# Tanh for Sigmoid, softmax steps spread over two blocks, and three transposes moved from DMA to TensorE, in a fused attention and channel-mix kernel

## The chip, the cores and the metric

One Trainium2 chip, one core of it. The metric is device microseconds (us) of one execution; lower is better. Engines are named as in the profile: PE is TensorE (matmul; PEld its weight loads), DVE is VectorE, ACT is ScalarE, POOL is GpSimd, SP is SyncE, which here only issues DMAs.

## The reference

Two operations, one after the other, for 4 batches of 6208 rows with 256 channels (tau is 1).

```python
qn = q / (norm(q, axis=1) + 1e-6)            # per channel, over the rows
kn = k / (norm(k, axis=1) + 1e-6)
s = kn.transpose(0, 2, 1) @ qn / tau         # 256 x 256 for each batch
a = exp(s - s.max(-1)); a /= a.sum(-1) + 1e-9
x = v @ a
x_prev = x shifted by one row, zero in front
xk = mu_k * x + (1 - mu_k) * x_prev
xr = mu_r * x + (1 - mu_r) * x_prev
kk = maximum(xk @ w_k, 0) ** 2               # 256 -> 1024
out = 1 / (1 + exp(-(xr @ w_r))) * (kk @ w_v)
```

The softmax of a batch needs all rows of q and k of that batch; the rest goes row by row.

## The kernel before

The rows of a batch are 12 blocks of 512 and 64 rows left over. The left-over rows of all batches form a 49th block at the end. Two kinds of work run beside each other.

**Covariance.** q and k of a batch are loaded in groups of 4 units (a unit is 128 rows); the 64 left-over rows are a group of one unit, group 0. `unit_matmul` adds a unit to the 256 x 256 sum `s_ps` with two matmuls (L133). `group_norms` adds the squares of a group (`qk2`) to the channel sums `ssq_ps`, with four matmuls of 32 columns side by side (L145). Batch 0 is loaded as f32 on SP's queue (L102), cast by VectorE (L113) and squared by ScalarE (L115). Later batches are cast to bf16 by the DMA, issued from GpSimd's queue (L107), and squared by ScalarE (L120). In the trace, `qk_392` and the like on ScalarE are such squares.

**Softmax chain** (`softmax_pieces`), once per batch: `copies` (ssq out of PSUM, L161), `gather` (four matmuls into `bank`, L168, then ScalarE's Sqrt into `rn`, L170), `evac` (s_ps out of PSUM, L185), `invert` (reciprocal of rn and a diagonal `rq_d`, L173 to L176), `spread` (matmul of rq_d with ones, L182), `scale` (L188), `exp` (ScalarE, L197), `weigh` (row sums inverted, `a_sb` written, L202 and L204).

**Channel mix**, block by block. A block's v is loaded as bf16 from GpSimd's queue (`v_load`, L223) and transposed by a DMA from SP's queue (`v_transpose`, L230) into `vT`. `x_half` makes half of the transposed x (L247), which ScalarE copies out (L249). VectorE makes the difference to the row before (`delta`, L279) and the two mixtures `xk` and `xr` (L289). `up` is the projection to 1024 in eight steps (L304) with a Relu on ScalarE (L307), `square` squares it on VectorE (L313), `down` makes gate and projection for 128 rows (L328, L332) in two halves, `finish` applies Sigmoid on ScalarE (L340) and multiplies on VectorE (L341).

The order on every engine is that of the code; nothing is reordered. Ahead of the loop stand all units of batch 0, its chain, the loads of the weights and the first units of batch 1. The loop runs over i from -2 and over eight steps j: in block i stand `down` of block i, `up` of block i + 1, and `x_half` and the mixtures of block i + 2, with v transposed for block i + 4 and loaded for i + 5. Units of the next batch stand at certain steps, and a chain is taken up piece by piece, one piece a step, as soon as its batch is complete:

```python
if chain:
    chain.pop(0)()
...
if j in ((5, 7) if i == -2 else (1, 3, 4, 5, 7)) and ...:
    unit(0 if i < -1 else 2)
```

Every wait of an instruction holds all that stand behind it on the same engine or queue. PSUM tiles are shared by tag: `kT_ps` has three buffers, `vr_ps` two, `xT_ps` one; `v_bf` has five buffers, `vT` four.

Of the kernel before, what the change touches and what calls it, by code (L numbers as in the profile page):

```python
# [18 lines left out]
def kernel(  # L19
# [13 lines left out]
    nc = tc.nc  # L33
# [32 lines left out]

    mu_k_t = const.tile([P, 2], F32, name="mu_k_t")
# [13 lines left out]
    def sizes(b):  # L81
        return [1] + [S] * (NB - 1) + ([S // 2] * 2 if b == 0 else [S])

# [38 lines left out]
    def unit_matmul(b, g, s, late=False):  # L122
        rows, n = rows_of(b, g)
        t0 = g == 0
        te = g == len(sizes(b)) - 1 and s == n - 1
        if t0:

            cov[b] = (ps.tile([P, 2, C], F32, name="s_ps", tag="s_ps" if b else "vr_ps", bufs=1 if b else 2),
                      ps.tile([P, 2 * C], F32, name="ssq_ps", tag="ssq_ps" if b else "vr_ps", bufs=1 if b else 2))
        s_ps = cov[b][0]  # L130
        qk = groups[b, g][0]
        for ih in range(2):
            nc.tensor.matmul(s_ps[:, ih, :], qk[:rows, s, 1, ih * P:(ih + 1) * P],  # L133
                             qk[:rows, s, 0, :], start=t0 and ih == 0, stop=te,
                             skip_group_check=True)
        if s == n - 1 and not late:
            group_norms(b, g)

    def group_norms(b, g):
# [4 lines left out]
        for u in range(n):  # L144
            nc.tensor.matmul(ssq_ps[32 * u:32 * (u + 1)], ones[:rows, :32],  # L145
                             qk2[:rows, u].rearrange("p i c -> p (i c)"),
                             start=g == (1 if u else 0), stop=g == len(sizes(b)) - 1, tile_position=(0, 32 * u),
                             skip_group_check=True)

    def softmax_pieces(b):  # L150
# [12 lines left out]
        def gather():  # L163
# [6 lines left out]
            nc.scalar.activation(rn, bank[:, C:C + 4], AF.Sqrt)  # L170

        def invert():
            nc.vector.tensor_scalar_add(rn, rn, 1e-6)  # L173
            nc.vector.reciprocal(rn, rn)
            for h in range(2):
                nc.vector.tensor_scalar_mul(rq_d[:, h * P:(h + 1) * P], ident_f, rn[:, h:h + 1])  # L176
            if inv_tau != 1.0:
                nc.vector.tensor_scalar_mul(rk, rk, inv_tau)
# [26 lines left out]


        return [copies, gather, evac, invert, spread, scale] + ([] if bounded else [top]) + [exp, weigh]


# [16 lines left out]
    def v_transpose(i):  # L226
# [4 lines left out]
        st[i, "vT"] = vT  # L231

# [102 lines left out]
    def finish(i, s):  # L335
# [4 lines left out]
        nc.scalar.activation(res[:, s], vr_ps[:, D:], AF.Sigmoid)  # L340
        nc.vector.tensor_tensor(res[:, s], res[:, s], vr_ps[:, :D], op=OP.mult)  # L341
# [11 lines left out]
    for g in range(len(sizes(0))):  # L353
# [4 lines left out]
        if g == NB - 5:  # L358
            nc.sync.dma_start(mu_k_t, moe_mu_k.rearrange("(h p) -> p h", p=P))
            nc.sync.dma_start(mu_r_t, moe_mu_r.rearrange("(h p) -> p h", p=P))  # L360
# [43 lines left out]

    next_load()
    next_load()
    nc.gpsimd.dma_start(w_k_sb, moe_w_k.rearrange("(ko ki) f -> ki ko f", ki=P))
# [3 lines left out]
    nc.gpsimd.dma_start(w_v_sb, moe_w_v.rearrange("(fo fi) d -> fi fo d", fi=P))  # L411
    next_load()
    v_load(2)
    v_transpose(0)
    v_transpose(1)
# [15 lines left out]
    for u in early:  # L431
        unit_square(*u)
    group_norms(*early[0][:2])
    pos["sq"] += S
    pos["mm"] += S

# [3 lines left out]
    for i in range(-2, NBLK):  # L440
        for j in range(8):
# [7 lines left out]
            if chain:  # L449
                chain.pop(0)()  # L450
# [24 lines left out]
            if j == 5 and 2 <= i + 4 < NBLK - 1:  # L475
                v_transpose(i + 4)
            b = (i + 2) // NB
            if j in ((5, 7) if i == -2 else (1, 3, 4, 5, 7)) and pos["mm"] < len(units) and units[pos["mm"]][0] <= b + 1:
                unit(0 if i < -1 else 2)
# [41 lines left out]
```

## Time and profile before

| | |
|---|---|
| median of 3 runs | 558.94 us (558.53 to 561.2) |
| profiled execution | 563.61 us, its span 561.8 us |
| TensorE busy | 511.9 us (91%), mean granted clock 0.965 |
| ScalarE busy | 451.1 us (80%) |
| VectorE busy | 408.4 us (73%) |
| GpSimd busy | 98.2 us (17%) |
| DMA | 84.55 MB, mean 150 GB/s |

The span goes from the first to the last instruction; about 1.8 us of the profiled execution lie outside. A row of the timeline has the start, the length, the engine, the line, the operation with what it writes and reads, how many of them were merged, and in brackets the idle time ahead of it and what ended it. In a row of groups stand, behind the bar, the busy time in all and the mean in ns of one instruction. A row of a DMA issue ends with the time from issue to landing.

### The profile page before, as it was taken

The numbers are of one execution on the slowest core, as the hardware profiler recorded it, in microseconds if no ns is written. First come the engines' busy times: TensorE is split into PE (matmuls) and PEld (weight loads), VectorE is DVE, ScalarE is ACT, GpSimd is POOL, SyncE is SP. The second block draws the span as 40 slices with busy tenths as digits, with TensorE's granted clock in tenths as the row PEclk, the third lists the DMA queues.
The fourth block names the chain that finished last, engine by engine and source line by source line (L and its number), as shares of the span: only waits on it lengthen the run. The fifth ranks groups of instructions, "written<-read, shape, count | busy, mean of one in ns | idle before, by whom it ended". The sixth has DMA issues, their size and how long they took to land. (4 is left out here: it accounts for less than half of the span.)

```text
span 561.8 us, 9979 instructions
## 1 busy us (share of the span) xinstructions
PE 511.9 (91%) x3502; PEld 333.8 (59%) x3560; DVE 408.4 (73%) x953; ACT 451.1 (80%) x897; POOL 98.2 (17%) x140
## 2 busy tenths in 40 slices
PE   4765679999988999999988999999989999999996
PEld 1331346666655666666655666666655666666665
DVE  3552637787758777777778777777778898888984
ACT  6773768888868898888888898889879777878774
POOL 0045413124210213222310213221001010000000
PEclk9785979999989999999999999999999999999999
DMA  8989999979992699899992699899643768534122
GB/s 289 402 253 180 191 176 169 198 126 141 185 164 56 124 179 167 132 199 141 183 182 57 98 206 163 132 194 155 123 85 76 144 104 133 108 84 114 37 76 95
DMA packets 147426, 84.55 MB, mean 150 GB/s; under 512 B 55408, under 2 KB 143792, under 8 KB 147376
## 3 DMA queue, kind: packets, MB, share of 16 engines
q0 software_dynamic: 65808, 33.01, 48.7%
q1 hardware_dynamic: 81568, 50.90, 38.1%
q8 instruction: 28, 0.46, 0.4%
q14 instruction: 22, 0.18, 0.1%
HBM read 78.71 MB, written 25.43 MB: 185 GB/s over the span
## 5 line engine op out<-in xcount | busy, mean ns | idle before, releaser
L307 ACT ACTIVATE kr<-kT_ps 128x512 bf16<-128x512 f32 (+1 forms) x392 | 232.7, 596 | 46.4 <-PE kT_ps L304 31.9
L332 PE MATMUL vr_ps<-w_v_sb,kk 128*128 128x256 bf16 x1552 | 234.7, 274 | 4.2 <-DVE kk L313 2.1
L304 PE MATMUL kT_ps<-xk,w_k_sb 128*128 128x512 bf16 (+1 forms) x726 | 221.4, 380 | 2.3 <-ACT kr L307 1.6
L332 PEld LDWEIGHTS <-kk 128*128 128x128 bf16 x1552 | 152.4, 98 | 62.4 <-DVE kk L313 3.8
L313 DVE TENSOR_TENSOR kk<-kr 128x512 bf16<-128x512 bf16 (+1 forms) x392 | 155.4, 415 | 5.9 <-ACT kr L307 5.3
L341 DVE TENSOR_TENSOR res<-res,vr_ps 128x256 f32<-128x256 f32 x194 | 81.2, 419 | 90.6 <-ACT res L340 88.9
L304 PEld LDWEIGHTS <-w_k_sb 128*128 128x128 bf16 x784 | 73.9, 99 | 40.4 <-issue 12.4
L249 ACT CAST xT<-xT_ps 128x512 bf16<-128x512 f32 x95 | 55.9, 589 | 42.8 <-PE xT_ps L247 42.8
L133 PE MATMUL s_ps<-qk 128*128 128x256 bf16 (+1 forms) x392 | 75.6, 297 | 15.9 <-DVE qk L113 14.6
L328 PE MATMUL vr_ps<-w_r_sb,xr 128*128 128x256 bf16 x388 | 74.5, 274 | 4.0 <-DVE res L341 3.3
L340 ACT ACTIVATE res<-vr_ps 128x256 f32<-128x256 f32 x194 | 74.1, 382 | 3.1 <-PE vr_ps L332 2.3
L289 DVE SCALAR_TENSOR_TENSOR xr<-delta,mu_r_t,xT 128x512 bf16<-128x512 bf16 x96 | 71.4, 744 | 0.0
L289 DVE SCALAR_TENSOR_TENSOR xk<-delta,mu_k_t,xT 128x512 bf16<-128x512 bf16 x96 | 71.4, 744 | 0.0
L247 PE MATMUL xT_ps<-vT,a_sb 128*128 128x512 bf16 x192 | 58.4, 388 | 11.4 <-DMA vT<-v_bf 11.4
L328 PEld LDWEIGHTS <-xr 128*128 128x128 bf16 x388 | 38.2, 98 | 49.7 <-issue 6.5
L107 POOL DMA_DIRECT2D qk<-in_q_dram x39 | 28.9, 741 | 221.9 <-ACT qk_3346 L120 31.3
L133 PEld LDWEIGHTS <-qk 128*128 128x128 bf16 (+1 forms) x392 | 39.4, 105 | 30.9 <-DVE qk L113 19.7
L223 POOL DMA_DIRECT2D v_bf<-in_v_dram x48 | 36.4, 761 | 118.5 <-DMA vT<-v_bf 99.5
L279 DVE TENSOR_TENSOR delta<-xT 128x1024 bf16<-128x1024 bf16 x48 | 33.3, 693 | 17.0 <-ACT xT L249 16.9
L107 POOL DMA_DIRECT2D qk<-in_k_dram x39 | 28.9, 742 | 4.9 <-DMA w_v_sb<-in_moe_w_v_dram 2.9
L247 PEld LDWEIGHTS <-a_sb 128*128 128x128 bf16 x192 | 19.0, 100 | 15.8 <-issue 13.4
L145 PEld LDWEIGHTS <-ones 128*32 128x32 bf16 (+1 forms) x196 | 5.7, 94 | 14.7 <-issue 14.7
(193 smaller groups left out, 236.4 us busy)
## 6 DMA issues: line engine op xcount, KB each, us to landing
out_dram<-res SPq DMA_DIRECT2D x48, 512.0 KB, 3.9
v_bf<-in_v_dram POOLq DMA_DIRECT2D x48, 256.0 KB, 7.9
qk<-in_q_dram POOLq DMA_DIRECT2D x36, 256.0 KB, 5.6
qk<-in_k_dram POOLq DMA_DIRECT2D x36, 256.0 KB, 6.9
vT<-v_bf SPq DMA_TRANSPOSE x48, 5.6
f_110<-in_q_dram SPq DMA_DIRECT2D x1, 512.0 KB, 4.0
f_112<-in_k_dram SPq DMA_DIRECT2D x1, 512.0 KB, 5.1
f_132<-in_q_dram SPq DMA_DIRECT2D x1, 512.0 KB, 5.8
```

What stands on the lines that cost most here:

```text
L107: nc.gpsimd.dma_start(qk[:rows, :n, i, :], qk_src(t, b, g))
L133: nc.tensor.matmul(s_ps[:, ih, :], qk[:rows, s, 1, ih * P:(ih + 1) * P], qk[:rows, s, 0, :], start=t0 and ih == 0, stop=te, skip_group_che ...
L247: nc.tensor.matmul(xT_ps, a_sb[:, b, ih, dh * P:(dh + 1) * P], vT[:, :, ih, :], start=ih == 0, stop=ih == 1)
L249: (nc.vector.tensor_copy if first else nc.scalar.copy)(xT[:, dh, 1:], xT_ps)
L289: nc.vector.scalar_tensor_tensor(o[:, dh], st[i, "d"][:, dh], mu[:, dh:dh + 1], st[i, "x"][:, dh, :M], op0=OP.mult, op1=OP.add)
L304: nc.tensor.matmul(kT_ps[:, :m], w_k_sb[:, dh, fh * P:(fh + 1) * P], xk[:, dh, :m], start=dh == 0, stop=dh == 1)
L307: nc.scalar.activation(kr[:, :m], kT_ps[:, :m], AF.Relu)
L313: nc.vector.tensor_tensor(st[i, "kk"][:, fh, :m], kr[:, :m], kr[:, :m], op=OP.mult)
L328: nc.tensor.matmul(vr_ps[:, D:], xr[:, dh, s * P:(s + 1) * P], w_r_sb[:, dh, :], start=dh == 0, stop=dh == 1)
L332: nc.tensor.matmul(vr_ps[:, :D], kk[:, fh, s * P:(s + 1) * P], w_v_sb[:, fh, :], start=fh == 0, stop=fh == 7)
L340: nc.scalar.activation(res[:, s], vr_ps[:, D:], AF.Sigmoid)
L341: nc.vector.tensor_tensor(res[:, s], res[:, s], vr_ps[:, :D], op=OP.mult)
```

## The change

- The gate is made with Tanh: sigmoid(z) = (1 + tanh(z/2)) / 2. `finish` has Tanh on ScalarE and (res + 1) * vr in one scalar_tensor_tensor on VectorE; the factor 1/2 goes into w_v_sb, halved once by VectorE in block -1 of the loop.
- For batches 1 to 3 the root leaves ScalarE: VectorE copies the four columns of `bank` to `rn`, GpSimd raises them to 0.5. The chain of these batches has 16 steps instead of 8, seven or eight of them empty.
- v of blocks 0, 1 and 2 is transposed by eight TensorE transposes each, into a PSUM tile of the tag `kT_ps`, and copied out by VectorE, ScalarE and VectorE.
- Batch 0 loads its groups in the order 1, 2, 0, 3, ...; the two small mu loads go out first, from ScalarE's queue. On GpSimd's queue w_k goes ahead of the first group of batch 1, and one group fewer is loaded there ahead of the loop; v of block 2 stands ahead of the third.
- Ahead of the steady loop stand 7 units of batch 1 instead of 12; blocks 0 to 7 have six units instead of five.

```diff
+    half = const.tile([P, 4], F32, name="half")
+    nc.vector.memset(half, 0.5)
...
-            nc.scalar.activation(rn, bank[:, C:C + 4], AF.Sqrt)
+            if b == 0:
+                nc.scalar.activation(rn, bank[:, C:C + 4], AF.Sqrt)
+
+        def roots():
+            nc.vector.tensor_copy(rn, cov[b][:, C:C + 4])
+
+        def roots2():
+            nc.gpsimd.tensor_tensor(rn, rn, half, op=OP.pow)
...
+        return [copies, None, gather, roots, roots2, evac, None, invert, None, spread, None, scale,
+                None if bounded else top, exp, None, weigh]
...
+    def v_transpose_pe(i, evac):
+        v_bf = st.pop((i, "v"))
+        vT_ps = ps.tile([P, S, 2, P], BF16, name="vT_ps", tag="kT_ps", bufs=3)
+        for s in range(S):
+            for h in range(2):
+                nc.tensor.transpose(vT_ps[:, s, h], v_bf[:, s, h * P:(h + 1) * P], ident)
+        def go():
+            vT = p2.tile([P, S, 2, P], BF16, name="vT", tag="vT", bufs=4)
+            evac(vT, vT_ps)
+            st[i, "vT"] = vT
+        return go
...
-        nc.scalar.activation(res[:, s], vr_ps[:, D:], AF.Sigmoid)
-        nc.vector.tensor_tensor(res[:, s], res[:, s], vr_ps[:, :D], op=OP.mult)
+        nc.scalar.activation(res[:, s], vr_ps[:, D:], AF.Tanh, scale=0.5)
+        nc.vector.scalar_tensor_tensor(res[:, s], res[:, s], 1.0, vr_ps[:, :D], op0=OP.add, op1=OP.mult)
...
-    for g in range(len(sizes(0))):
+    nc.scalar.dma_start(mu_k_t, moe_mu_k.rearrange("(h p) -> p h", p=P))
+    nc.scalar.dma_start(mu_r_t, moe_mu_r.rearrange("(h p) -> p h", p=P))
+    for g in order(0):
...
-    v_transpose(0)
-    v_transpose(1)
...
     evac()
+    go = v_transpose_pe(0, nc.vector.tensor_copy)
     invert()
     spread()
+    go()
     unit(0)
-    early = units[pos["mm"]:pos["mm"] + S]
-    for u in early:
-        unit_matmul(*u, late=True)
     for f in rest:
         f()
     for h in range(2):
         x_half(0, h)
-    for u in early:
-        unit_square(*u)
-    group_norms(*early[0][:2])
...
+    v_transpose_pe(1, nc.scalar.copy)()
+    for _ in range(S):
+        unit(0)
...
+            if i == -1 and j == 6:
+                v_transpose_pe(2, nc.vector.tensor_copy)()
+                nc.vector.tensor_scalar_mul(w_v_sb, w_v_sb, 0.5)
...
+            if i < -1:
+                slots = ()
+            elif i == -1:
+                slots = (5, 7)
+            elif i < 8:
+                slots = (1, 2, 3, 4, 5, 7)
+            else:
+                slots = (1, 3, 4, 5, 7)
```

What this makes of the order on the engines is shown at three places. First ScalarE from the dummy Exp of batch 0's chain (`gate`) into block -1, before:

```order
L419 ACTIVATE gate<-ones 128x1
L120 ACTIVATE qk_388<-qk 64x512
L197 ACTIVATE s_sb,sm<-s_sb,rn 128x256 x2
L249 CAST xT<-xT_ps 128x512
L120 ACTIVATE qk_392<-qk 128x512 x4
L120 ACTIVATE qk_399<-qk 128x512 x2
L307 ACTIVATE kr<-kT_ps 128x512
L249 CAST xT<-xT_ps 128x512
```

and in the changed kernel:

```order
L448 ACTIVATE gate<-ones 128x1
L127 ACTIVATE qk_391<-qk 64x512
L211 ACTIVATE s_sb,sm<-s_sb,rn 128x256 x2
L281 CAST xT<-xT_ps 128x512
L261 COPY vT<-vT_ps 128x1024
L127 ACTIVATE qk_397<-qk 128x512 x4
L339 ACTIVATE kr<-kT_ps 128x512
L281 CAST xT<-xT_ps 128x512
```

The copy of block 1's vT now stands ahead of the first relu (`kr`), and two of the six squares ahead of it have moved behind.

Second, VectorE in block -1, around the last squares of block 0 (`kk`); before:

```order
L289 SCALAR_TENSOR_TENSOR xk<-delta,mu_k_t,xT 128x512
L313 TENSOR_TENSOR kk<-kr 128x512 x2
L289 SCALAR_TENSOR_TENSOR xr<-delta,mu_r_t,xT 128x512
L313 TENSOR_TENSOR kk<-kr 128x512
L241 COPY xT<-xT 128x2
```

and in the changed kernel:

```order
L345 TENSOR_TENSOR kk<-kr 128x512
L261 COPY vT<-vT_ps 128x1024
L504 TENSOR_SCALAR w_v_sb<-w_v_sb 128x2048
L345 TENSOR_TENSOR kk<-kr 128x512
L321 SCALAR_TENSOR_TENSOR xr<-delta,mu_r_t,xT 128x512
L345 TENSOR_TENSOR kk<-kr 128x512
L273 COPY xT<-xT 128x2
```

The copy of block 2's vT and the halving of w_v stand ahead of the last two squares of block 0.

Third, VectorE in the chain of batch 1, from the first to the middle step; before, all in one piece of the loop:

```order
L161 COPY ssq<-ssq_ps 128x512
L313 TENSOR_TENSOR kk<-kr 128x512
L289 SCALAR_TENSOR_TENSOR xk<-delta,mu_k_t,xT 128x512
L313 TENSOR_TENSOR kk<-kr 128x512
L289 SCALAR_TENSOR_TENSOR xk<-delta,mu_k_t,xT 128x512
L341 TENSOR_TENSOR res<-res,vr_ps 128x256
L185 COPY s_sb<-s_ps 128x512
L313 TENSOR_TENSOR kk<-kr 128x512
L173 TENSOR_SCALAR rn<-rn 128x4
L174 RECIPROCAL rn<-rn 128x4
L176 TENSOR_SCALAR rq_d<-ident_f,rn 128x128 x2
```

and in the changed kernel, from the copy of the four columns on:

```order
L181 COPY rn<-bank 128x4
L345 TENSOR_TENSOR kk<-kr 128x512
L311 TENSOR_TENSOR delta<-xT 128x1024
L374 SCALAR_TENSOR_TENSOR res<-res,vr_ps 128x256
L345 TENSOR_TENSOR kk<-kr 128x512
L321 SCALAR_TENSOR_TENSOR xk<-delta,mu_k_t,xT 128x512
L199 COPY s_sb<-s_ps 128x512
L345 TENSOR_TENSOR kk<-kr 128x512
L321 SCALAR_TENSOR_TENSOR xk<-delta,mu_k_t,xT 128x512
L374 SCALAR_TENSOR_TENSOR res<-res,vr_ps 128x256
L345 TENSOR_TENSOR kk<-kr 128x512
L187 TENSOR_SCALAR rn<-rn 128x4
```

Between the copy of `rn` (L181) and its next use (L187) now stand ten other instructions of VectorE, and GpSimd's root. Before, `rn` came from ScalarE, behind a table load. On GpSimd's queue the root stands between the v loads of blocks 12 and 13:

```order
L114 DMA qk<-in_k_dram 128x4x256
L241 DMA v_bf<-in_v_dram 128x4x256
L184 TENSOR_TENSOR rn<-rn,half 128x4
L241 DMA v_bf<-in_v_dram 128x4x256 x3
L114 DMA qk<-in_q_dram 128x4x256
```

ScalarE's row has 16 table loads before and three in the changed kernel, the last of them for the dummy Exp of batch 0's chain.

More of the change, by code (lines that the diff above doesn't have):

```diff
@@ L82, in sizes, with order @@
         return [1] + [S] * (NB - 1) + ([S // 2] * 2 if b == 0 else [S])
+    def order(b):
+        g = list(range(len(sizes(b))))
+        return [1, 2, 0] + g[3:] if b == 0 else g
     def rows_of(b, g):
@@ L123, in unit_matmul @@
         rows, n = rows_of(b, g)
-        t0 = g == 0
+        t0 = g == order(b)[0] and s == 0
         te = g == len(sizes(b)) - 1 and s == n - 1
@@ L403, in next_load @@
         pos["ld"] += 1
+    nc.gpsimd.dma_start(w_k_sb, moe_w_k.rearrange("(ko ki) f -> ki ko f", ki=P))
     next_load()
-    next_load()
-    nc.gpsimd.dma_start(w_k_sb, moe_w_k.rearrange("(ko ki) f -> ki ko f", ki=P))
     v_load(1)
@@ L449 @@
             if chain:
-                chain.pop(0)()
+                piece = chain.pop(0)
+                if piece is not None:
+                    piece()
             if 0 <= i + 1 < NBLK:
```

22 lines of the change are left out of this document (9 added, 13 removed).

## Prediction

> **What bounds the kernel now.** I read the busy totals, then the table of busy time by stretch, then TensorE's timeline at the places where that table shows gaps.
>
> ```profile
> span 561.8 us, 9979 instructions
> PE 511.9 (91%) x3502; PEld 333.8 (59%) x3560; DVE 408.4 (73%) x953; ACT 451.1 (80%) x897; POOL 98.2 (17%) x140
> ```
>
> TensorE is idle for 49.9 of 561.8 us. Each row of the next table gives a stretch, its length, the busy time of PE, PEld, DVE, ACT and POOL, the granted clock, the DMA share and GB/s.
>
> ```profile
> 10.00:20.00 10.00, 7.53 (x54) 3.68 (x52) 5.55 (x8) 8.20 (x9) 0.00 (x0) 1.00 1.02 417
> ...
> 500.00:540.00 40.00, 39.79 (x278) 27.04 (x280) 34.97 (x83) 31.71 (x65) 0.00 (x0) 1.00 0.28 78
> ```
>
> Between 10 and 20 us the DMA engines are full (1.02, 417 GB/s): loading the first q and k sets the pace. Late in the program TensorE is busy 39.79 of 40 us at full clock: there it is the bound, and nothing done for another engine can help. What can be gained is idle or slow TensorE time, and it lies in the start-up and in the softmax chains.
>
> ```profile
> 46.50:52.20 5.70, 1.08 (x6) 0.47 (x4) 0.00 (x0) 0.00 (x0) 1.65 (x3) 0.50 1.33 181
> ...
> 66.60:73.10 6.50, 1.14 (x7) 0.68 (x7) 3.10 (x8) 2.47 (x5) 1.51 (x3) 0.91 1.45 160
> 73.10:78.80 5.70, 5.46 (x22) 2.57 (x23) 0.90 (x3) 3.97 (x6) 1.48 (x2) 0.51 1.39 188
> ```
>
> Two stretches with TensorE almost idle, and after the second one 5.46 us of work at a granted clock of 0.51. TensorE's timeline (start, length, then in brackets the idle time before and its releaser) names what it waited for:
>
> ```profile
> 45.69 1.89 PE L133 MATMUL s_ps<-qk 128*128 128x256 bf16 x8 [0.99 <-DMA qk<-in_k_dram]
> 52.21 1.86 PE L247 MATMUL xT_ps<-vT,a_sb 128*128 128x512 bf16 x4 [4.64 <-DMA vT<-v_bf]
> 54.43 2.14 PE L145 MATMUL ssq_ps<-qk_392,ones 128*32 128x512 bf16 x4 [0.35 <-ACT qk_392 L120]
> ...
> 57.32 1.06 PE L304 MATMUL kT_ps<-xk,w_k_sb 128*128 128x512 bf16 x2
> 59.83 0.59 PE L247 MATMUL xT_ps<-vT,a_sb 128*128 128x512 bf16 x2 [1.45 <-DMA vT<-v_bf]
> ...
> 66.62 0.59 PE L304 MATMUL kT_ps<-xk,w_k_sb 128*128 128x512 bf16 x2 [0.20 <-ACT kr L307]
> ...
> 73.12 1.01 PE L247 MATMUL xT_ps<-vT,a_sb 128*128 128x512 bf16 x2 [5.36 <-DMA vT<-v_bf]
> ```
>
> All three waits of the first blocks are for a DMA transpose. v itself is there long before:
>
> ```profile
> 36.44 0.87 POOL L223 DMA_DIRECT2D v_bf<-in_v_dram  x1
> ...
> 40.60 0.83 POOL L223 DMA_DIRECT2D v_bf<-in_v_dram  x1
> ```
> ```profile
> v_bf<-in_v_dram POOLq DMA_DIRECT2D x1, 256.0 KB, 4.1
> ```
> ```profile
> v_bf<-in_v_dram POOLq DMA_DIRECT2D x1, 256.0 KB, 10.1
> ```
> ```profile
> vT<-v_bf SPq DMA_TRANSPOSE x1, 11.6
> ```
>
> Issue to landing: v of block 0 lands at 36.4 + 4.1 = 40.5, its transpose needs 11.6 us more because the queues are full; v of block 1 lands at 50.7.
>
> The three later chains, one stretch each:
>
> ```profile
> 153.00:177.00 24.00, 19.60 (x117) 12.19 (x118) 16.59 (x42) 18.08 (x36) 3.17 (x5) 0.93 0.65 102
> ...
> 283.00:306.00 23.00, 19.47 (x129) 12.26 (x129) 17.70 (x44) 19.69 (x38) 2.22 (x3) 1.00 0.70 117
> ...
> 408.00:432.00 24.00, 20.48 (x136) 13.01 (x138) 18.16 (x46) 19.74 (x39) 1.48 (x2) 1.00 0.43 84
> ```
> ```profile
> 160.68 1.19 PE L182 MATMUL bank<-rq_d,ones_f 128*128 128x256 f32 x2 [2.22 <-DVE rq_d L176]
> ```
>
> TensorE loses 4.4, 3.5 and 3.5 us there, and the first one also 0.07 x 24 = 1.7 us of clock: 13.1 us in all. In the order of before, ScalarE's table loads stand inside these chains:
>
> ```profile
> L340 ACT ACT_TABLE_LOAD x7 | 9.0, 1283 | 0.1
> L170 ACT ACT_TABLE_LOAD x4 | 5.1, 1283 | 0.1
> L197 ACT ACT_TABLE_LOAD x3 | 3.8, 1283 | 0.1
> ```
>
> **The change part by part.** All in us of the profiled execution, 563.61 (span 561.8, 1.8 around it); the median of the runs, 558.94, is 4.7 lower, and the gains are taken from that.
>
> (1) Loads of the first phase, +1.5.
>
> ```profile
> 0.74 0.59 SPq L102 DMA_DIRECT2D f_95<-in_q_dram  x1
> ...
> 2.00 0.59 SPq L102 DMA_DIRECT2D f_110<-in_q_dram  x1
> ...
> 14.14 0.39 SPq L359 DMA_DIRECT2D mu_k_t<-in_moe_mu_k_dram  x1
> ```
>
> The first 512 KB load now goes out at 0.74 instead of 2.00: 1.26 us of a full pipe. The two 1 KB mu loads leave SP's queue, where each took one of the turns of a phase that the DMA bounds; they go out from ScalarE's queue before it has work. Nothing gained if the pipe fills no sooner, 3 if both come in full; I take 1.5, nearest to the head of the queue.
>
> (2) First up projection earlier, +2.9. The vT copy of block 0 (128x1024 from PSUM) stands on VectorE ahead of `scale`, and eight transposes on TensorE ahead of `spread`. A 128x128 transpose isn't in the trace. Below it costs a weight load; above, a 128x256 matmul at half clock, so eight at most the 1.89 us of the row at 45.69. I take 1.9, as this stretch has half clock. A bound for the copy comes from two rows (1024 elements from SBUF; 512 from PSUM, doubled):
>
> ```profile
> L113 DVE CAST qk<-f_110 128x1024 bf16<-128x1024 f32 x1 | 0.7, 694 | 2.1 <-DMA f_110<-in_q_dram 2.1
> ```
> ```profile
> L161 DVE COPY ssq<-ssq_ps 128x512 f32<-128x512 f32 x4 | 2.7, 685 | 1.0 <-PE ssq_ps L145 1.0
> ```
>
> 0.7 to 1.4; I take 1.2. Together they delay the chain by some 0.5:
>
> ```profile
> 45.72 0.62 DVE L204 TENSOR_SCALAR a_sb<-s_sb,sm 128x256 bf16<-128x256 f32 x2
> ```
> ```profile
> 53.74 2.19 ACT L120 ACTIVATE qk_392<-qk 128x512 bf16<-128x512 bf16 x4
> ...
> 66.93 1.13 ACT L307 ACTIVATE kr<-kT_ps 128x512 bf16<-128x512 f32 x2
> ```
>
> So a_sb is ready at 46.3 + 0.5 = 46.8, four xT matmuls (1.86) end at 48.7, eight transposes of block 1 at 50.6 (its v lands no later than 50.7, and now has one group less ahead of it). ScalarE copies that vT (1024 elements, as two relus: 1.1) to 51.7, then squares four units (2.19) to 53.9; the norms follow, and the first up projection starts at 54.4 instead of 57.32. The new wait: TensorE is in order, so these norms hold it where the transposes did.
>
> (3) Block -1 of the loop, +1.5. Before, 57.32 to 66.62, 9.3 us. Now ScalarE has 8 relus, 2 xT copies and 4 squares: 14 x 0.55 = 7.7. I take 7.8.
>
> (4) The wait for block 2's transpose, +5.4 (row at 73.12), and the slow clock after it, +2.0: 5.46 us at 0.51 are 2.7 too many, but the new start has a cold stretch of its own, so between 0 and 2.7.
>
> (5) VectorE in block -1, -1.5. The vT copy (1.2) and the halving of w_v_sb (2048 bf16 elements: between 0.35, the a_sb row of 256 elements below, and 2.8, eight times it; I take 1.4, twice the cast above) stand ahead of the last two squares of block 0. Behind them wait `kk`, then the second half of block 0's first down projection. Full cost 2.6, nothing if VectorE has run ahead.
>
> (6) Units deferred, -1.8. Twelve units were done before the steady loop, now seven; five move to blocks where TensorE is the bound. Two matmuls of a unit cost 1.89/4/2 = 0.24 at full clock, plus a quarter of four concurrent norms (at most 2.14/4 at half clock): 0.24 to 0.5, I take 0.35.
>
> (7) Block 3 is the first with a DMA transpose, -0.7. Its v goes out after w_v, v2 and two to three groups, lands near 61, and its transpose takes 9 to 12 us as above: 70 to 73, needed at about 71. Between 0 and 3.
>
> (8) The later chains, +9.5. The loads of tables go (three remain, all in the first chain), Sqrt leaves ScalarE, and each step now has one or two empty steps behind it, so a result is asked for 1 to 2 us later than before. VectorE's work stays:
>
> ```profile
> L341 DVE TENSOR_TENSOR res<-res,vr_ps 128x256 f32<-128x256 f32 x194 | 81.2, 419 | 90.6 <-ACT res L340 88.9
> ...
> L204 DVE TENSOR_SCALAR a_sb<-s_sb,sm 128x256 bf16<-128x256 f32 x8 | 2.5, 350 | 0.1
> L176 DVE TENSOR_SCALAR rq_d<-ident_f,rn 128x128 f32<-128x128 f32 x8 | 2.1, 334 | 0.1
> ...
> L294 DVE SCALAR_TENSOR_TENSOR xk<-delta,mu_k_t,xl 128x256 bf16<-128x256 bf16 x2 | 1.0, 476 | 0.0
> ```
>
> Per chain three 128x512 operations (0.685), two of 0.334, two of 0.350: 3.4, and 0.5 for eight gates. A block has 18 VectorE instructions, so the 83 between 500 and 540 are 4.6 blocks of 8.7 us with 12.6% spare: 2.2 in two blocks. It is 1.7 short; I leave 1.2 of loss per chain, as some of it fits into buffers. 13.1 - 3.6 = 9.5; at worst 6, at best 13.
>
> (9) The gate as scalar_tensor_tensor, -0.3. By 476 against 419 it costs 57 ns more, 194 times: 11 us of VectorE, beside TensorE's work. The other end is 2, if the last blocks (VectorE at 34.97 of 40) feel it. Tanh itself is one activation of the same shape. The root on GpSimd:
>
> ```profile
> masks.py:199 POOL TENSOR_SCALAR_AFFINE_SELECT ident<-ident 128x128 bf16<-128x128 bf16 x1 | 0.3, 288 | 0.1
> ```
>
> No pow stands in the trace; this row, with 32 times the elements, says 0.3, above I allow 4 and take 1. VectorE has about 4 us of other rows between writing `rn` and reading it back. The v loads behind it on GpSimd's queue lose their lead over the program, but are five blocks early.
>
> Sum: 1.5 + 2.9 + 1.5 + 5.4 + 2.0 - 1.5 - 1.8 - 0.7 + 9.5 - 0.3 = 18.5. The profiled execution would be 545.1, the median 540.4.
>
> The Trainium skill ("TensorE: Matmul & The Clock Gate", section "Part 4: PE-mode transpose") gives about 275 ns for such a transpose in one kernel and says that it does not bring up the full clock. By 275 ns the sixteen of blocks 0 and 1 would be an estimated 4.4 us instead of 3.8, the sum 0.6 less.
>
> **The rivals.**
> - Clock. The stretch at 0.51 shows TensorE slow for over 5 us of dense work after a pause. If the transposes don't count as work for the clock, block -1 runs at half speed: the 2.0 of step 4 and the 1.5 of step 3 go, 544. For it: 46.5 to 52.2 stood at 0.50. Against: that was an idle stretch, and ScalarE bounds block -1. The Trainium skill (same page and section as above) states this rule.
> - Transfers. Blocks now ask for data 12 us earlier, while the DMA share is 1.4 to 1.45. If vT of block 3 or 4 and the groups (six units a block instead of five) come as late as before, the 5.4 of step 4 is paid again: 546. Against: three transposes left the queues.
> - VectorE bounds the chains. If spreading saves only the table loads and each still costs 2.8, the gain is 4.7 instead of 9.5: 545.
> - Slower: pow. If it takes longer than the 4 us of cover, VectorE stops in order, `kk` comes late and TensorE with it, three times. To eat 18.5 it must take 4 + 6.2 = 10 us; at 12 us the result is 565. Against: all GpSimd rows that compute take 0.1 to 0.3 us.
> - That tables are loaded all the same is excluded by the order of the changed program, which holds three loads.
>
> **How the numbers follow.** My forecast 58%, clock 13%, transfers 12%, VectorE 13%, pow 4%. Less than 0.5% (2.8 us) cannot be told from no change. All but the last are faster, and I keep 2% for no change and 3% for slower: 0.95, 0.02, 0.03. Range: the best ends of steps 1, 4, 5 and 8 together reach 533; two of the milder rivals together give 549 to 550. 534 to 549.
>
> **What would show it.** Right: no wait for vT in the first three blocks, first up projection near 53, second block's near 60; no table load after the first chain; TensorE idle under 2 us in each chain. Wrong: a wait of several us at the fourth block's xT; a clock near 0.5 past 60 us; VectorE waiting for GpSimd before `rn`; idle TensorE in steady blocks, where 57 ns more per gate would be felt.

## The result, and the profile after

The changed kernel takes 539.25 us (median of 4 runs, 538.85 to 539.62), the kernel before beside it 558.74 us (4 runs, 558.46 to 561.2): a ratio of 0.9642, interval 0.9613 to 0.967. Forecast were 540.4 us and 534 to 549. The profiled execution of after took 539.62 us, 0.4 above the median of its runs; that of before lay 4.7 above (563.61 against 558.94).

The page of after begins:

```profile
span 537.8 us, 10013 instructions
PE 505.4 (94%) x3525; PEld 333.8 (62%) x3584; DVE 410.0 (76%) x960; ACT 434.9 (81%) x882; POOL 101.4 (19%) x143
```

TensorE is idle for 32.4 us of the span; before it was 49.9. ScalarE is 16.2 us less busy; thirteen table loads of 1.28 us that are gone (16 before, three now) would be 16.7, and a copy of vT is new.

**Start-up.** TensorE's timeline of after, at the rows that answer to those of before:

```profile
43.35 1.05 PE L175 MATMUL bank<-thirty_83,ssq 128*128 128x1 f32 x8 [0.79 <-DVE ssq L168]
44.26 0.61 PE L257 MATMUL vT_ps<-ident,v_bf 128*128 128x128 bf16 x8
...
51.42 1.06 PE L257 MATMUL vT_ps<-ident,v_bf 128*128 128x128 bf16 x8
...
55.98 0.60 PE L336 MATMUL kT_ps<-xk,w_k_sb 128*128 128x512 bf16 x2
...
60.20 0.61 PE L257 MATMUL vT_ps<-ident,v_bf 128*128 128x128 bf16 x8
...
62.72 0.59 PE L336 MATMUL kT_ps<-xk,w_k_sb 128*128 128x512 bf16 x2 [1.21 <-ACT kr L339]
63.80 0.59 PE L279 MATMUL xT_ps<-vT,a_sb 128*128 128x512 bf16 x2
64.23 0.59 PE L336 MATMUL kT_ps<-xk,w_k_sb 128*128 128x512 bf16 x2
...
74.66 0.59 PE L279 MATMUL xT_ps<-vT,a_sb 128*128 128x512 bf16 x2
```

No `xT` matmul waits for a transpose, not that of block 2 (63.80) nor that of block 3 (74.66), whose transpose is still a DMA. The gather of the norms (43.35), though, comes later than before, where it stood at 39.92. Of before, that row and the first one behind the wait for block 2's transpose:

```profile
39.92 1.05 PE L168 MATMUL bank<-thirty_83,ssq 128*128 128x1 f32 x8 [0.79 <-DVE ssq L161]
...
73.93 1.06 PE L304 MATMUL kT_ps<-xk,w_k_sb 128*128 128x512 bf16 x2
```

The table by stretch has the same columns as in the prediction:

```profile
46.50:52.20 5.70, 3.98 (x16) 1.66 (x16) 2.02 (x6) 2.20 (x6) 3.99 (x6) 0.50 1.42 191
52.20:57.30 5.10, 3.97 (x21) 1.85 (x21) 3.06 (x7) 3.78 (x7) 2.70 (x4) 0.96 1.46 197
57.30:60.00 2.70, 2.70 (x15) 1.31 (x14) 2.60 (x6) 2.70 (x7) 1.48 (x2) 1.00 1.46 195
138.60:150.10 11.50, 11.41 (x80) 7.72 (x78) 10.07 (x26) 7.87 (x17) 7.01 (x9) 1.00 0.89 145
150.10:158.80 8.70, 8.55 (x59) 5.58 (x58) 8.66 (x23) 7.47 (x18) 0.00 (x0) 1.00 1.33 199
270.20:280.70 10.50, 10.32 (x70) 6.85 (x69) 9.30 (x25) 7.47 (x15) 6.26 (x8) 1.00 1.11 175
280.70:290.80 10.10, 9.56 (x64) 6.25 (x64) 8.82 (x24) 7.96 (x19) 0.00 (x0) 1.00 1.03 157
```

The last four rows are the first two later chains: TensorE is idle for 0.24 and 0.72 us in them, at full clock, though VectorE is busy 8.66 of 8.70 us. The clock is full from the middle of the 50s on.

**Where the time went.** A good ruler is the moment at which SP issues the store of a block's output. Three of these rows of before and then of after (blocks 0, 18 and 22; the second chain lies between the last two):

```profile
86.34 0.41 SPq L345 DMA_DIRECT2D out_dram<-res  x1
...
276.97 0.37 SPq L345 DMA_DIRECT2D out_dram<-res  x1
...
321.06 0.37 SPq L345 DMA_DIRECT2D out_dram<-res  x1
```
```profile
74.61 0.42 SPq L378 DMA_DIRECT2D out_dram<-res  x1
...
259.91 0.37 SPq L378 DMA_DIRECT2D out_dram<-res  x1
...
300.57 0.37 SPq L378 DMA_DIRECT2D out_dram<-res  x1
```

Differences of such rows, in us:

| from store to store | before | after | gain |
|---|---|---|---|
| start to block 0 | 86.34 | 74.61 | 11.73 |
| 0 to 6 (deferred units) | 62.26 | 64.00 | -1.74 |
| 6 to 9 (chain 1) | 35.18 | 28.11 | 7.07 |
| 18 to 22 (chain 2) | 44.09 | 40.66 | 3.43 |
| 30 to 34 (chain 3) | 42.20 | 38.52 | 3.68 |
| all others, to the last store | 286.80 | 286.80 | 0.00 |

The sum is 24.2, as the spans have it (24.0). It is 4.7 more than the 19.5 between the medians. A slow start of the profiled execution of before is 3.2 of that, as the first experiment shows; the rest is not traced to a place.

### The profile page after: what moved, and what is told of

Same layout as the page of the kernel before. It is cut to its first block, busy times and chain, and to the rows that moved or that the text cites. A ratio compares the mean times of both kernels' runs of the same rounds, so it can differ in the third digit from the quotient of the medians.

```text
span 537.8 us, 10013 instructions
## 1 busy us (share of the span) xinstructions
PE 505.4 (94%) x3525; PEld 333.8 (62%) x3584; DVE 410.0 (76%) x960; ACT 434.9 (81%) x882; POOL 101.4 (19%) x143
## 4 chain that ended last, share of the span: by engine, by line
PE 84%; DMA 8%; DVE 3%; ACT 2%; issue 1%; POOL 0%; SPq 0%; ACTq 0%
PE vr_ps L364 31%; PE kT_ps L336 28%; PE vr_ps L360 8%; PE xT_ps L279 8%; PE s_ps L140 6%; PE ssq_ps L152 2%; DMA f_336<-in_k_dram 2%; DMA f_248<-in_k_dram 2%; DMA f_160<-in_k_dram 1%; DMA qk<-in_k_dram 1%; DMA mu_k_t<-in_moe_mu_k_dram 1%; DVE xk L321 1%; ACT kr L339 1%; DVE kk L345 1%; DVE res L374 1%
## 5 line engine op out<-in xcount | busy, mean ns | idle before, releaser
L336 PE MATMUL kT_ps<-xk,w_k_sb 128*128 128x512 bf16 (+1 forms) x725 | 218.9, 377 | 2.9 <-ACT kr L339 1.2
L374 DVE SCALAR_TENSOR_TENSOR res<-res,vr_ps 128x256 f32<-128x256 f32 x194 | 81.5, 420 | 74.8 <-ACT res L373 72.5
L336 PEld LDWEIGHTS <-w_k_sb 128*128 128x128 bf16 x784 | 73.3, 98 | 37.7 <-issue 10.5
L140 PE MATMUL s_ps<-qk 128*128 128x256 bf16 (+1 forms) x392 | 75.1, 295 | 17.9 <-DVE qk L120 17.2
```

What stands on the lines that cost most here:

```text
L336: nc.tensor.matmul(kT_ps[:, :m], w_k_sb[:, dh, fh * P:(fh + 1) * P], xk[:, dh, :m], start=dh == 0, stop=dh == 1)
L374: nc.vector.scalar_tensor_tensor(res[:, s], res[:, s], 1.0, vr_ps[:, :D], op0=OP.add, op1=OP.mult)
```

## The experiments

**The kernel before, once more.** No edit.

> The kernel before, unchanged, for a second profile of it: the first profiled execution took 563.6 us where the median was 558.7, and the start times of its output stores show 7.1 us gained at the first of the later chains, but 3.4 and 3.7 at the other two. Theory: about 3 of the 4.9 us too many lie in the first of the later chains (a clock drop and a longer wait there), and a second profile shows that chain losing 3 to 4 us like the others, total near 558.7. Rival: the 4.9 us lie in the start-up, where the clock changes, and that chain loses 6 us again.

560.35 us, span 558.6. Its stores of blocks 0, 18 and 22:

```profile
83.14 0.40 SPq L345 DMA_DIRECT2D out_dram<-res  x1
...
273.72 0.37 SPq L345 DMA_DIRECT2D out_dram<-res  x1
...
317.80 0.37 SPq L345 DMA_DIRECT2D out_dram<-res  x1
```

Block 0 comes 3.20 us earlier than in the first profile; from 18 to 22 it is 44.08 against 44.09, and no stretch of the table behind block 0 differs by more than 0.1. The two executions differ in the start-up alone; the chains cost the same in both. The seven kernels of this document that have the chains of after (after itself, the five with other first loads, the one with DMA transposes) agree as well: 28.09 to 28.11, 40.66 to 40.67 and 38.51 to 38.73 us for the three chains. So a chain is read from one profile to about 0.2 us, while an edit to the start-up needs medians.

**DMA transposes for blocks 0 to 2 again.**

```diff
+    v_transpose(0)
+    v_transpose(1)
...
-    go = v_transpose_pe(0, nc.vector.tensor_copy)
...
-    v_transpose_pe(1, nc.scalar.copy)()
...
-                v_transpose_pe(2, nc.vector.tensor_copy)()
...
-            if j == 5 and 3 <= i + 4 < NBLK - 1:
+            if j == 5 and 2 <= i + 4 < NBLK - 1:
                 v_transpose(i + 4)
```

> The changed kernel with v of blocks 0, 1 and 2 transposed by DMA again, all else as changed. By steps 2 to 5 of the prediction the transposes are worth 2.9 + 1.5 + 5.4 + 2.0 - 1.5 = 10.3 us: 547 to 551, with waits of several us for vT ahead of the xT matmuls. Rival (transfers reordered in the queue do most of it, since v of block 2 now goes out ahead of the third group): 541 to 544.

543.1 us (541.94 to 544.03, 4 runs), 3.9 over after; ratio to before 0.9681 (0.9635 to 0.9727). TensorE's timeline has the waits back; its gather and its first row behind the wait for block 2 stand around them:

```profile
41.73 1.05 PE L175 MATMUL bank<-thirty,ssq 128*128 128x1 f32 x8 [0.79 <-DVE ssq L168]
...
51.21 1.87 PE L279 MATMUL xT_ps<-vT,a_sb 128*128 128x512 bf16 x4 [4.50 <-DMA vT<-v_bf]
...
66.74 0.78 PE L279 MATMUL xT_ps<-vT,a_sb 128*128 128x512 bf16 x2 [2.97 <-DMA vT<-v_bf]
67.32 1.06 PE L336 MATMUL kT_ps<-xk,w_k_sb 128*128 128x512 bf16 x2
```

With a third wait of 0.20 they sum to 7.7 us (11.4 in before), and the store of block 0 comes 4.6 later than in after: a wait taken away here is worth little more than half of its length. That other work then waits in its place is the likely reason, not one that a run shows.

The time lies where the rival put it, and the rival's mechanism shows in part: v of block 2 goes out at 45.14 us here and at 48.98 in before, and the wait for its transpose is 2.97 instead of 5.36 us. From the gather to the row behind that wait it is 34.01 us in before, 25.59 here and 20.88 in after. So of the 13.1 us gained in this piece, 8.4 came without the transposes, with the other edits ahead of the loop: the order on GpSimd's queue, one group and five units fewer. No run moves these one by one. Without the transposes the whole change still gains 17.9 us (561.03 for before beside it).

**Where the two small mu loads go.** Five kernels. First, mu back in the middle of SP's queue, the new group order kept:

```diff
-    nc.scalar.dma_start(mu_k_t, ...)
-    nc.scalar.dma_start(mu_r_t, ...)
...
+        if g == NB - 5:
+            nc.sync.dma_start(mu_k_t, ...)
+            nc.sync.dma_start(mu_r_t, ...)
```

> The changed kernel with the two mu loads back in the middle of SP's queue. Theory (slots): in the changed kernel SP's seventh and ninth load wait until the two slow mu loads have landed (5.1 and 6.5 us), because all hardware queues share a ring of completion slots; without them ahead of it SP goes on after six loads as fast as the loads land: last cast of batch 0 1.5 to 2.5 us earlier than 39.0, result 536.5 to 538. Rival (group order): the loss comes from the large group first; nothing gained, 539 to 539.5.

Then mu at the start as in after, but from GpSimd's queue (`nc.gpsimd.dma_start`):

> The changed kernel with the two mu loads at the very start, but issued from GpSimd's queue. Slots theory: SP's queue no longer waits for them, last cast 1.5 to 2.5 us earlier, 536 to 538. Rival (packets): the 4-byte packets themselves hold the DMA engines at the start whoever issues them, and the time stays at 538.5 to 539.5.

The old group order, mu at the start on ScalarE's queue (`order(b)` returns `g`, and the flag that starts the sum of the norms follows):

> The changed kernel with batch 0's groups in their old order 0, 1, 2, ..., the mu loads still first on ScalarE's queue. Slots theory: SP still waits for the mu loads, nothing gained or up to 0.8 lost, 539 to 540. Rival (group order): the old order alone gives back the 1.4 us that the loads are late, 537 to 538.

Mu on SP's queue behind the last load of batch 0:

> The changed kernel with the two mu loads behind the last load of batch 0 on SP's queue; they are wanted only by the mixtures of block 0, near 52 us. Packets theory (the 544 small packets hold the DMA engines for 1 to 2 us of a phase that the DMA bounds, wherever in it they stand): out of that phase they cost nothing, last cast of batch 0 ends 0.5 to 1 us before the 37.6 of the kernel with them in the middle, result 535.5 to 537, no worse than 536.8. Rival (place in the phase doesn't matter, only the wait at its head): as with them in the middle, 536.8.

Old order and mu in the middle of SP's queue, both edits undone:

> The changed kernel with both of its edits to the first loads undone: groups of batch 0 in the old order, the two mu loads in the middle of SP's queue. Each undone alone gave 537.7 (order) and 536.8 (mu). If both act on the same thing (the small packets of mu standing ahead of or beside the first large loads), this gives 536.5 to 537.5, no better than the mu edit alone. If they add, 535 to 536. If the new order is worth the 1.26 us that the earlier first full load suggests, once mu is out of the way, it gives 538, about 1.2 over the mu edit alone.

| group order | mu loads | median us (runs) | ratio to before |
|---|---|---|---|
| new (after) | first, ScalarE's queue | 539.25 (538.85 to 539.62, 4) | 0.9613 to 0.967 |
| new | first, GpSimd's queue | 539.37 (538.27 to 539.98, 4) | 0.9569 to 0.9637 |
| old | first, ScalarE's queue | 537.74 (537.5 to 538.47, 4) | 0.9546 to 0.9611 |
| old | middle, SP's queue | 537.62 (536.45 to 538.09, 6) | 0.9558 to 0.9619 |
| new | end, SP's queue | 537.1 (536.51 to 537.39, 6) | 0.9549 to 0.9611 |
| new | middle, SP's queue | 536.84 (535.98 to 538.6, 5) | 0.9535 to 0.9603 |

The median of before lay between 558.74 and 561.44 in the sets of runs behind this table, so the cleanest pair is mu from GpSimd's queue against mu in the middle, both with the new order and side by side on one chip: 2.5 us. The stretch from 4 to 8 us, of after, of mu from GpSimd's queue and of mu in the middle:

```profile
4.00:8.00 4.00, 0.00 (x0) 0.00 (x0) 1.39 (x2) 1.79 (x2) 0.00 (x0) 1.00 0.74 257
```
```profile
4.00:8.00 4.00, 1.01 (x5) 0.73 (x6) 1.39 (x2) 2.11 (x2) 0.00 (x0) 1.00 0.95 274
```
```profile
4.00:8.00 4.00, 0.82 (x4) 0.57 (x5) 1.65 (x3) 2.37 (x3) 0.00 (x0) 1.00 1.01 360
```

257 or 274 GB/s against 360: with mu at the start, whichever queue issues it, four microseconds carry some 0.3 to 0.4 MB less, about 1 us of a full pipe. The two loads are 1 KB each, but the page lists them as 544 packets, and in after they need 5.1 and 6.5 us to land.

SP also waits 1.2 + 0.9 us for their completions before it issues two later group loads; that a shared ring is the reason, as the first expectation says, no run shows. This wait does not explain the loss: from GpSimd's queue SP never waits for mu, and the time is the same. With the new order, mu at the start costs 2.4 us (539.25 against 536.84); with the old order, where a small group goes first, nothing that can be told (537.74 against 537.62). Between the orders with mu in the middle lie 0.8 us (537.62 and 536.84), with ranges that overlap. That small packets hold the DMA engines is a reading that fits, not one that a run isolates, and two results limit it. With mu at the end, behind the whole phase, nothing more is gained than in its middle (537.1 and 536.84), so inside the phase the same packets cost nothing that can be told. And with the old order the stretch from 4 to 8 us carries 314 GB/s with mu at the start and 357 without, yet no time is lost. The kernel with the new order and mu in the middle, 536.84, is faster than before and after: its highest run, 538.6, lies below the lowest of after, 538.85, though the two were not run side by side.

**Chain packed again:** its ten pieces in ten steps running, root still on GpSimd, Tanh kept.

```diff
-        return [copies, None, gather, roots, roots2, evac, None, invert, None, spread, None, scale,
-                None if bounded else top, exp, None, weigh]
+        return [copies, gather, roots, roots2, evac, invert, spread, scale] + ([] if bounded else [top]) + [exp, weigh]
```

> The changed kernel with the later chains in ten consecutive steps, without the empty ones; Tanh and the root on GpSimd stay. Theory (the distance between steps matters): VectorE comes to the scaled diagonal 1 to 2 us after the copy, ahead of GpSimd's 1.03 us, and TensorE waits at the first and the second small matmul, 1.5 to 3 us a chain: 544 to 548. Rival (the table loads were the whole cost): under 0.7 us a chain, 539 to 541.

541.7 us (541.53 to 541.93, 4 runs), 2.45 over after; ratio to before 0.9663 (0.9625 to 0.9701). TensorE now waits for `invert`:

```profile
147.15 0.70 PE L196 MATMUL bank<-rq_d,ones_f 128*128 128x256 f32 x2 [1.75 <-DVE rq_d L192]
```

By the stores the three chains cost 1.66, 0.39 and 0.50 more than in after, of a gain of 7.07, 3.43 and 3.68. Spacing the steps is the small part. (Ten pieces in 16 steps leave six empty, not seven or eight, and no piece has two empty steps behind it.) The result lies between the two expectations, nearer to that of the tables.

**Tanh alone in the kernel before.** The gate and the halving of w_v_sb, nothing else; 9 table loads.

```diff
-        nc.scalar.activation(res[:, s], vr_ps[:, D:], AF.Sigmoid)
-        nc.vector.tensor_tensor(res[:, s], res[:, s], vr_ps[:, :D], op=OP.mult)
+        nc.scalar.activation(res[:, s], vr_ps[:, D:], AF.Tanh, scale=0.5)
+        nc.vector.scalar_tensor_tensor(res[:, s], res[:, s], 1.0, vr_ps[:, :D], op0=OP.add, op1=OP.mult)
...
+            if i == -1 and j == 6:
+                nc.vector.tensor_scalar_mul(w_v_sb, w_v_sb, 0.5)
```

> The kernel before with one part of the change alone: the gate as Tanh and scalar_tensor_tensor, w_v_sb halved once in block -1. Chains, roots and start-up as before; 9 table loads in the program instead of 14, no more spacing. If a table load in a chain costs TensorE about 1 us (11 loads fewer went with about 11 us of the 13.7 us that the three chains gained, the packed chain having shown that spacing is worth 0.85 a chain), five fewer give about 5 us, less 1.4 for the halving in the start-up: 3.5 to 5 under the kernel before, the gain at the chains. If loads cost nothing unless they stand together with close-packed steps (the steps of the chain wait for each other anyway), the gain is 0 to 1 us. If the gate by scalar_tensor_tensor were dearer (476 instead of 419 ns), blocks between chains would grow; the changed kernel's row (420) says they don't.

553.99 us (552.68 to 556.33, 4 runs) against 560.97 for before beside it; ratio 0.9884 (0.9835 to 0.9933). The gain, 7.0 us, is larger than expected. The expectation counted 14 loads in the kernel before, whose lists have 16: seven are gone, not five. The chains give 2.41, 1.98 and 1.98 us, for two loads fewer in each.

**After with Sigmoid.** The gate edit undone with the halving of w_v_sb, all else kept: the chain spread, the root on GpSimd, 10 table loads.

> The changed kernel with the gate by Sigmoid and a plain product again (w_v_sb not halved); chain spread, roots on GpSimd: 10 table loads instead of 3. By about 1 us a load: 7 us slower than the changed kernel, 545 to 547, with 2 to 2.5 us lost at each later chain. By the rival (spread steps leave so much room that a load of 1.28 us on ScalarE is hidden, and only packed chains feel loads): 539 to 541.

546.96 us (546.14 to 548.27, 4 runs), as the price of 1 us a load said; ratio to before 0.976 (0.9721 to 0.9799). ScalarE's timeline in the second chain, then VectorE's and TensorE's:

```profile
284.60 1.28 ACT L211 ACT_TABLE_LOAD   x1
285.89 0.51 ACT L211 ACTIVATE s_sb<-s_sb,rn 128x256 f32<-128x256 f32 x1
...
287.48 1.28 ACT L373 ACT_TABLE_LOAD   x1
288.78 0.38 ACT L373 ACTIVATE res<-vr_ps 128x256 f32<-128x256 f32 x1
```
```profile
289.19 0.42 DVE L374 TENSOR_TENSOR res<-res,vr_ps 128x256 f32<-128x256 f32 x1 [3.89 <-ACT res L373]
```
```profile
289.67 0.38 PE L360 MATMUL vr_ps<-w_r_sb,xr 128*128 128x256 bf16 x2 [1.56 <-DVE res L374]
```

This is how a table load gets to TensorE: Exp's load, the exponentials, a Relu and the load for Sigmoid delay the next gate; VectorE, in order, stands idle for 3.89 us at its product; TensorE waits behind it for a buffer of `vr_ps`, 1.56 us. This kernel loses 2.84 us against after in each of the two later chains.

**After with Sigmoid and Sqrt on ScalarE.** As above, and the root as an activation from `bank`: 16 table loads, as many as before (not two more), the chain still spread.

```diff
-            nc.vector.tensor_copy(rn, cov[b][:, C:C + 4])
+            nc.scalar.activation(rn, cov[b][:, C:C + 4], AF.Sqrt)
...
-            nc.gpsimd.tensor_tensor(rn, rn, half, op=OP.pow)
+            pass
```

> As the kernel with Sigmoid and the spread chain, and the root again as Sqrt on ScalarE: 16 table loads, two more than the kernel before, but the chain spread over 16 steps. By about 1 us a load: 13 us slower than the changed kernel, 551 to 553, hardly any gain at the chains against the kernel before. By the rival (the spread hides the loads): 540 to 543, which would give the spacing what the removed tables were credited with.

554.17 us (553.16 to 555.02, 4 runs), ratio to before 0.9886 (0.9847 to 0.9924): slower than even the price of 1 us a load said. The six kernels side by side, by the stores of the second and third chain (us from block 18 to 22, and from 30 to 34):

| chain | loads in it | packed | spread |
|---|---|---|---|
| Sigmoid, Sqrt on ScalarE | 4 | 44.09, 42.20 (before) | 46.30, 44.07 |
| one of the two replaced | 2 | 42.11, 40.22 (Tanh alone) | 43.50, 41.36 (Sigmoid) |
| Tanh, root on GpSimd | 0 | 41.05, 39.02 | 40.66, 38.52 (after) |

The two parts don't add. With four loads the spread chain is 2.0 us **worse** than the packed one; with none it is 0.45 better. A load costs 1.4 us in the spread chain, more than its own 1.28, and 0.5 to 1.0 in the packed one. (The granted clock was 0.96 in the stretch of 46.30 us and 1.00 in the others; the third chain, all at 1.00, gives the same 1.4.) VectorE's idle time ahead of gates behind loads in the second chain shows it, first of before, then of this kernel:

```profile
289.56 0.42 DVE L341 TENSOR_TENSOR res<-res,vr_ps 128x256 f32<-128x256 f32 x1 [2.64 <-ACT res L340]
...
300.51 0.42 DVE L341 TENSOR_TENSOR res<-res,vr_ps 128x256 f32<-128x256 f32 x1 [0.85 <-ACT res L340]
```
```profile
279.93 0.42 DVE L374 TENSOR_TENSOR res<-res,vr_ps 128x256 f32<-128x256 f32 x1 [3.55 <-ACT res L373]
...
295.13 0.42 DVE L374 TENSOR_TENSOR res<-res,vr_ps 128x256 f32<-128x256 f32 x1 [3.89 <-ACT res L373]
```

The second rows are the gates behind the exponentials. In the packed chain VectorE has `weigh` to do while Sigmoid's table comes back, in the spread one nothing: that the empty step behind `exp` is the reason fits them, but no run moved that step alone. The first rows, behind the two loads around Sqrt, differ by 0.9 us too, and for those it is no reason.

**Nine powers in a row on GpSimd,** to see where the root stops being free.

```diff
+    two = const.tile([P, 4], F32, name="two")
+    nc.vector.memset(two, 2.0)
...
+            for _ in range(4):
+                nc.gpsimd.tensor_tensor(rn, rn, half, op=OP.pow)
+                nc.gpsimd.tensor_tensor(rn, rn, two, op=OP.pow)
             nc.gpsimd.tensor_tensor(rn, rn, half, op=OP.pow)
```

> The changed kernel with nine powers instead of one in each later chain (0.5 and 2 in turn, same values), 9 x 1.03 = 9.3 us on GpSimd. In the changed kernel VectorE asks for the result 4.8 us after it is there, so up to 5.8 us are covered and 3.5 us a chain are late: 5 to 10 us more in all, 544 to 550. If something else fills the gap, or buffers hide the lateness, under 2 us more: 541.

557.37 us (555.06 to 558.36, 8 runs), 18.1 over after and well above the 544 to 550 expected; ratio to before 0.9937 (0.9905 to 0.9969). The powers take 10.5 us; VectorE, then TensorE, wait for them:

```profile
150.95 0.17 DVE L192 TENSOR_SCALAR rn<-rn 128x4 f32<-128x4 f32 x1 [4.58 <-POOL rn L189]
```
```profile
151.91 1.22 PE L201 MATMUL bank<-rq_d,ones_f 128*128 128x256 f32 x2 [4.35 <-DVE rq_d L197]
```

The chains lose 6.67, 5.54 and 5.99 us, more than VectorE's wait of 4.58; why more, no run shows. The slower rival's mechanism is real, and its point lies near where the prediction had it: a root of 10 us was to eat the whole gain, and powers of 10.5 us leave 1.4 of 19.5 (3.7 against the runs of before beside it). One power takes a tenth of that.

## Why the prediction was right, point by point

The mechanism came as forecast: the waits for vT are gone, the later chains have no table load, and TensorE hardly idles in them. That the time came within 1.2 us of the forecast is in part luck. 24.2 us were gained against the profile and 18.5 forecast; two terms were off by 4 to 5 us each, in opposite directions, and the profile of before lay 4.7 above its median. Later sets of 9 to 17 runs put before at 560.97 to 561.44 us; from there the same 18.5 would have given 542.5 to 542.9. Against the profile that the prediction started from:

| step | predicted | measured | from |
|---|---|---|---|
| 1, loads | +1.5 | -3.4 | gather 39.92, now 43.35 |
| 2, first up projection | +2.9 | +4.8 | gather to first up 17.40, now 12.63 |
| 3 and 5, block -1 | 0 | +2.6 | first up to that of the next block 9.30, now 6.74 |
| 4, wait for block 2's vT | +5.4 | +5.8 | 66.62 to 73.93, now 62.72 to 64.23 |
| 4, clock behind it | +2.0 | +2.0 | 73.93 to the store at 86.34, now 64.23 to 74.61 |
| 6, units deferred | -1.8 | -1.7 | stores 0 to 6 |
| 7, block 3's transpose | -0.7 | 0 | no wait at 74.66 |
| 8, chains | +9.5 | +14.2 | the three stretches of stores |
| 9, gate and root | -0.3 | 0 | all other stretches equal |

**Step 1 failed in its sign.** "They go out from ScalarE's queue before it has work" priced the mu loads by the turn they take in a queue, and put at nothing what they do to the transfers beside them at the start. VectorE's timeline has the last cast and the copy of the last norms of batch 0; of after:

```profile
39.02 0.67 DVE L120 CAST qk<-f_377 128x512 bf16<-128x512 f32 x1
42.60 0.69 DVE L168 COPY ssq<-ssq_ps 128x512 f32<-128x512 f32 x1 [2.92 <-PE ssq_ps L152]
```

Of before:

```profile
37.57 0.57 DVE L113 CAST qk<-f_375 128x512 bf16<-128x512 f32 x1
39.17 0.69 DVE L161 COPY ssq<-ssq_ps 128x512 f32<-128x512 f32 x1 [1.03 <-PE ssq_ps L145]
```

Casts end 1.6 us later (39.69 against 38.14), and 1.9 more pass until the norms are there (2.91 against 1.03). Not all of this is the change's. The five kernels of the experiments that begin with the same loads as after have the gather between 40.81 and 42.23, three with mu on SP's queue at 39.41, 40.65 and 41.11; the profile of after is the latest of all. The 1.9 us go with the granted clock from 36 to 40 us, 0.50 in after and 1.00 with mu in the middle of SP's queue. But it is 0.50 with mu at the end as well, in a kernel that takes 537.1 us, so no run ties this clock to the mu loads. The medians size the step better: 539.25 us against 537.62 with both edits to the first loads undone, a loss of 1.6 where a gain of 1.5 was forecast.

The start-up as a whole, steps 1 to 5 and 7, came out close (11.7 against 11.1) only because steps 2, 3 and 5 were underestimated, and because the profile of before had a start 3.2 us longer than the second one. Against that second profile the start-up gains 8.5, of which the medians show some 7: 19.5 less 14.2 for the chains plus 1.7 for the units. The transposes alone are 3.9 of these, by the medians.

**Step 8 was mis-sized.** It left 1.2 us of loss in each chain, since VectorE was 1.7 us short of room. That balance took 476 ns for the gate's new form:

```profile
L374 DVE SCALAR_TENSOR_TENSOR res<-res,vr_ps 128x256 f32<-128x256 f32 x194 | 81.5, 420 | 74.8 <-ACT res L373 72.5
```

420, as the plain product had (419). And VectorE being full for two blocks doesn't hold TensorE, which idles for 0.24 and 0.72 us. The gain is even 1.1 above the 13.1 us of idle time and clock that the three stretches showed.

A part of chain 1's 7.07 is not the chain's. Before still had two units of batch 1 in this stretch (four matmuls into `s_ps`, 0.76 us, and four for the norms, 0.40), which after does in blocks 0 to 6, where step 6 pays for them. And the granted clock in its first two blocks, 1.00 in after, was lower in before:

```profile
148.60:161.90 13.30, 10.55 (x70) 6.92 (x70) 9.63 (x25) 9.80 (x19) 4.45 (x6) 0.95 1.13 167
161.90:175.90 14.00, 12.29 (x73) 7.48 (x73) 9.02 (x23) 11.18 (x23) 0.00 (x0) 0.92 0.34 71
```

The kernel with Sigmoid and Sqrt on ScalarE has no unit there either and a clock of 1.00, with all four loads in a spread chain: it gains 1.69 us in chain 1 and loses 2.21 and 1.87 in the others. So some 3.7 of the 7.07 go with units and clock rather than with tables or spacing; what sets this clock no run shows.

The prediction credited tables and spacing together. In the two later chains, where no unit moved and the clock is 1.00 before and after, the packed chain without loads gains 6.2 of 7.1 us (3.04 of 3.43 and 3.18 of 3.68); spacing with the tables still in place loses time. Over all three it is 11.6 of 14.2 (121.47 us in before, 109.84 there, 107.29 in after).

**Steps 2, 3 and 5.** The copies of vT and the halving took 0.68 and 0.69 us, not 1.2 and 1.4, and ScalarE's copy 1.01:

```profile
45.46 0.68 DVE L261 COPY vT<-vT_ps 128x1024 bf16<-128x1024 bf16 x1
...
62.73 0.69 DVE L504 TENSOR_SCALAR w_v_sb<-w_v_sb 128x2048 bf16<-128x2048 bf16 x1
```

Eight transposes took 0.61 us at full clock and 1.06 in the slow stretch, against 1.9. No wait for `kk` stands in TensorE's timeline of block 0 behind them. Step 4 came out near its size, but by the DMA-transpose kernel the wait for block 2 would have shrunk from 5.36 to 2.97 us without a transpose on TensorE.

**Step 9.** GpSimd's root and the rows of VectorE around it, in the first later chain:

```profile
141.61 1.04 POOL L184 TENSOR_TENSOR rn<-rn,half 128x4 f32<-128x4 f32 x1 [15.78 <-DVE rn L181]
```
```profile
147.48 0.39 DVE L187 TENSOR_SCALAR rn<-rn 128x4 f32<-128x4 f32 x1
```

It takes 1.04 us, the value taken, and is done 4.8 us before VectorE reads it.

**The rivals.** Clock: it did not come, 0.96 between 52.2 and 57.3 us and 1.00 from there on, with eight transposes just ahead (51.42) and eight behind (60.20). Whether transposes count as work for the clock no run shows, as matmuls stand around them. By 275 ns a piece, the figure that the Trainium skill ("TensorE: Matmul & The Clock Gate", "Part 4: PE-mode transpose") has from one kernel, eight would be an estimated 2.2 us; here, issued back to back, they take 0.61. Transfers: false, no wait at 74.66. VectorE as the bound of the chains: false, as above. Root too long: not here, but shown to work as described. Of the signs that the prediction named, the first up projections came at 55.98 and 62.72 instead of near 53 and 60: the gather is 4.9 us later than step 1 had it, less the 1.9 that step 2 did better.

## What to carry to other kernels

Count the table switches inside a latency chain before anything else: here each was worth 0.5 to 1.4 us of the bounding engine, and taking them out of a packed chain gave 6.2 of the 7.1 us that the two later chains gained. Take the loads out before spreading the steps: spread with four loads was worse than packed with four (46.30 against 44.09 us). Test the two edits apart, since they need not add. Try tiny strided loads later than the first microseconds of a phase that the DMA bounds. And don't credit an edit with the whole wait that went: undo it alone, as other edits may have shortened the same wait.

## What the runs showed of the hardware

- Behind block 0 the two profiled executions of the kernel before agree to 0.1 us in 470 (470.53 and 470.48); their 3.2 us of difference lie in the start-up. A granted clock of 0.50 or 1.00 for the same stretch of the start-up (36 to 40 us) came with first loads that cost the same (537.1 and 536.84 us).
- A scalar_tensor_tensor on 128x256 f32 with an operand in PSUM costs what a tensor_tensor does, 420 against 419 ns, though one on bf16 in SBUF takes 476 for as many elements.
- A table load is 1.28 us, and the next activation starts 0.01 us after it (284.60 and 285.89 above). The Trainium skill ("ScalarE: Activation LUTs", "What ACT_TABLE_LOAD costs") adds 1.38 us of drain to a switch; no row here shows it.
- Two 1 KB loads in 544 packets, at the start of a phase that the DMA bounds, cost 2.4 us in one order of the loads (539.25 against 536.84) and nothing measurable in another (537.74 against 537.62).
- A power of 128x4 f32 on GpSimd takes 1.0 us; of nine in a row two took 1.27 and 1.51.
